# A planned lead-in: maxima taken by readiness, other TensorE times in the task list, dense groups let in earlier

## The chip, the cores and the metric

The kernel runs on one core of a Trainium2 chip. The metric is the device time of one execution in microseconds (us). The kernel before was run three times: 1574.43 us is the median, the runs lie between 1574.12 and 1575.43. One further execution was taken with the hardware profiler; its trace is what the views below show.

## What is computed

The input x has 2048 tokens of 512 numbers. One branch is attention in which 32 heads of 16 numbers share one key and one value head; the other is a feed-forward layer with the Mish function. All of it is in fp32.

```python
def _A_ref(x, wq, wk, wv, wo):                       # x: [1, 2048, 512]
    q = (x @ wq).reshape(B, S, H, Dh).transpose(0, 2, 1, 3)     # H = 32, Dh = 16
    k = x @ wk                                       # [1, 2048, 16], one for all heads
    v = x @ wv
    scores = jnp.einsum("bhqd,bkd->bhqk", q, k) * (Dh ** -0.5)
    p = _softmax(scores, axis=-1)
    o = jnp.einsum("bhqk,bkd->bhqd", p, v)
    return o.transpose(0, 2, 1, 3).reshape(B, S, H * Dh) @ wo
def _B_ref(x, w1, b1, w2):                           # 512 -> 1792 -> 512
    h = x @ w1 + b1
    return (h * jnp.tanh(softplus(h))) @ w2
xn = _layernorm(x)
return x + _A_ref(xn, wq, wk, wv, wo) * _silu(_B_ref(xn, w1, b1, w2))
```

## The kernel before

**Pieces.** The tokens are cut into four chunks of 512. A chunk's x is normalized, transposed by TensorE (tiles xp, L303), copied by ScalarE (xf), and projected to keys and values in four passes (kp, L341). ScalarE writes the high part of the keys, VectorE adds the low part (k_low, L238); from then on the chunk's keys are ready. ScalarE then copies the values (vt, L355), TensorE transposes them (vp, L360), and VectorE puts them in place. The queries come as 32 groups v of four heads times 512 queries, eight groups to a chunk.

**The loop.** It has 512 steps, one for each query group and tile of 128 keys. In a step TensorE makes four tiles of scores (e, L1056) which ScalarE turns into exponentials (pt, L1058), and it multiplies the exponentials of two steps ago with the values (four pv matmuls, L1143). The softmax needs the maximum of each query beforehand: for a later query group TensorE makes four further products (m, L1078), in each of which VectorE takes the maximum along 512 keys (mb, L1082). A query group has 32 *pairs* of these (one product from the upper and one from the lower half of the array's rows), and the maxima run LEAD = 20 steps ahead of the scores. When a group's 32 pairs are done, c_rows (L1097) reduces them and SyncE moves the result into the queries' spare rows with eight small DMAs (L1122); the group's scores need them.

**Dense work.** The query projection, the feed-forward layer and the output projection are cut into *groups*: a chain of matmuls into one bank of PSUM (xps), then a copy by ScalarE (hb, L763, for the feed-forward layer), which GpSimd works on. There is one such bank, so one group must be copied out before the next may begin. Within the loop a matmul is run as an upper and a lower row half (L120), up to eight halves in one step; ahead of the loop it is run whole (L116). A group can begin only when its weights have arrived and are split into high and low parts. Steps that find no group ready have no dense work.

**The lead-in.** What stands ahead of the loop is laid out when the program is built. A list of tasks (engine, assumed duration, what it depends on) is put into `plan`. Each engine has a clock T, and again and again the option that can start earliest is taken and its instructions are written out. For TensorE the options are a task from the list (x_transpose with an assumed 0.6 us at L1343, a pass of k_proj with 0.9 at L1378, v_transpose with 0.5 at L1389), "M" (one pair of maxima), or, if neither can start within 0.35 us, "X": three matmuls of a dense group. A new dense group is let in only while fewer than 1 + (s - 18) / X_US have begun at the assumed time s (L1480), and only when the copy of the last one has been written out; if none may begin, "X" is one warm-up matmul (keep_warm, L1393) that nobody reads. The copy of a finished group is itself a ScalarE task, put at 0.35 us after the group's last matmul (put_off, L1274). After "M" TensorE's clock is moved on by 0.25 or 0.45 (L1465).

Which pair "M" takes is a fixed list, MSEQ (L65): eight pairs of query group 0, two of group 1, the other 24 of group 0, the other 30 of group 1. m_ready (L1398) looks at the next entry only: its queries must have been moved, its chunk's keys be ready and a bank free. m_need (L69) says after how many pairs of the list a query group is complete. The loop begins once group 0's rows are moved and 40 pairs are done (L1454).

## Time and profile before

| what | value |
|---|---|
| median of three runs | 1574.43 us |
| the profiled execution's own span | 1575.7 us |
| TensorE (PE) busy | 1563.1 us, 99% of the span |
| VectorE (DVE) busy | 1352.7 us, 86% |
| ScalarE (ACT) busy | 1300.4 us, 83% |
| GpSimd (POOL) busy | 642.2 us, 41% |
| first score matmul of the loop | 82.58 us after the span's start |

A busy share is a mean over the lead-in, the loop and the end. A matmul's end is modelled, so a busy TensorE need not be one at its peak. PE is TensorE's matmuls, PEld its weight loads, SPq the DMA queue of SyncE. "Granted clock" is the share of TensorE's full clock that the chip gave it in a stretch. In the rows below, a bracket at the end of a row is the wait before it and the instruction that ended the wait.

### The profile page before, as it was taken

What the parts mean: (1) busy time and instruction counts of PE and PEld (TensorE: products, weight loads), DVE (VectorE), ACT (ScalarE), POOL (GpSimd) and SP (SyncE); (2) the same over time, 40 slices, a digit from 0 to 9 for tenths busy, and PEclk for the clock granted to TensorE, in tenths of its full rate; (3) what the DMA queues carried; (4) which work ended last, traced back from release to release, by engine and by line L of the source; (5) the groups of instructions that cost most, each with busy time, mean ns of one, the idle gap of its engine ahead of it and who ended that gap; (6) DMA issues with size and microseconds to landing.
All of it is one profiled execution on the core that took longest, in us unless ns stands there. A gap on an engine that the chain in (4) does not pass through costs nothing.

```text
span 1575.7 us, 32007 instructions
## 1 busy us (share of the span) xinstructions
PE 1563.1 (99%) x11905; PEld 846.9 (54%) x11905; DVE 1352.7 (86%) x2307; ACT 1300.4 (83%) x2501; POOL 642.2 (41%) x668
## 2 busy tenths in 40 slices
PE   8999999999999999999999999999999999999998
PEld 5555555555555555555555555555555555555555
DVE  7898888988989888898998988889889998888852
ACT  6488888798998778878888787887898879788876
POOL 4677376175474203604425042260442415225222
PEclk9999999999999999999999999999999999999999
DMA  6223132142331304122131311221413221031110
GB/s 196 94 85 118 52 102 104 42 141 85 111 103 46 110 20 143 51 69 75 31 102 51 125 58 43 85 70 38 144 59 105 59 94 65 19 111 32 48 44 29
DMA packets 75082, 124.45 MB, mean 79 GB/s; under 512 B 21744, under 2 KB 36336, under 8 KB 74928
## 3 DMA queue, kind: packets, MB, share of 16 engines
q1 hardware_dynamic: 74784, 122.29, 24.8%
q8 instruction: 94, 1.54, 0.4%
q14 instruction: 60, 0.49, 0.1%
q10 hardware_dynamic: 144, 0.13, 0.0%
HBM read 74.65 MB, written 26.21 MB: 64 GB/s over the span
## 4 chain that ended last, share of the span: by engine, by line
PE 96%; DVE 1%; ACT 1%; DMA 0%; issue 0%; SPq 0%; POOL 0%; DVEq 0%; ACTq 0%
PE xps L120 43%; PE pv L1143 32%; PE e L1056 10%; PE m L1078 7%; PE kp L341 1%; PE xps L116 1%; PE pv L1136 1%; DVE mb L1082 1%; PE e L1029 1%; PE tail L120 0%; PE tailx L120 0%; DMA xin<-in_dram 0%; ACT pt L1058 0%; ACT pt L1033 0%; PE tail L1231 0%
## 5 line engine op out<-in xcount | busy, mean ns | idle before, releaser
L1082 DVE TENSOR_REDUCE mb<-m 128x1 f32<-128x512 f32 x2048 | 1273.8, 683 | 168.7 <-PE m L1078 124.9
L1058 ACT ACTIVATE pt<-e 128x512 f32<-128x512 f32 x1978 | 1038.3, 601 | 215.3 <-PE e L1056 208.9
L1078 PE MATMUL m<-ks,qt 48*128 48x512 f32 (+1 forms) x2048 | 844.5, 422 | 0.7 <-DVE mb L1082 0.3
L1056 PE MATMUL e<-qt,ks 64*128 64x512 f32 x1978 | 722.4, 398 | 0.1
L1143 PE MATMUL pv<-pt,vaug 128*32 128x512 f32 x3968 | 528.5, 605 | 0.0
L1078 PEld LDWEIGHTS m<-ks,qt 48*128 48x128 f32 (+1 forms) x2048 | 373.5, 185 | 60.3 <-DVE mb L1082 18.1
L1056 PEld LDWEIGHTS e<-qt,ks 64*128 64x128 f32 x1978 | 367.5, 186 | 5.2 <-ACT pt L1058 1.1
L120 PE MATMUL xps<-xt,ws 64*128 64x512 f32 x1224 | 338.8, 409 | 0.0
L120 PE MATMUL xps<-wbs,act 64*128 64x512 f32 x1248 | 336.9, 407 | 0.1
L120 PEld LDWEIGHTS xps<-xt,ws 64*128 64x128 f32 x1224 | 210.9, 185 | 196.9 <-ACT pt L1058 129.1
L120 PEld LDWEIGHTS xps<-wbs,act 64*128 64x128 f32 x1248 | 217.7, 185 | 172.4 <-ACT pt L1058 109.1
L174 POOL TENSOR_SCALAR t<-t 128x512 f32<-128x512 f32 x56 | 34.4, 614 | 328.1 <-ACT t L771 327.8
L1143 PEld LDWEIGHTS pv<-pt,vaug 128*32 128x32 f32 x3968 | 78.1, 108 | 132.2 <-issue 124.0
L164 POOL TENSOR_TENSOR hb<-hb,t 128x512 f32<-128x512 f32 x56 | 72.3, 1290 | 97.1 <-ACT t L784 73.9
L120 PE MATMUL xps<-xt,wq 64*128 64x512 f32 x336 | 93.0, 410 | 0.0
L120 PEld LDWEIGHTS xps<-xt,wq 64*128 64x128 f32 x336 | 57.9, 185 | 54.1 <-ACT pt L1058 34.4
L120 PE MATMUL xps<-wbs,ot_all 64*128 64x512 f32 x288 | 79.5, 409 | 0.0
L120 PEld LDWEIGHTS xps<-wbs,ot_all 64*128 64x128 f32 x288 | 49.6, 184 | 46.7 <-ACT pt L1058 29.3
L164 POOL TENSOR_TENSOR hb<-hb,u 128x512 f32<-128x512 f32 x56 | 72.3, 1291 | 4.4
L164 POOL TENSOR_TENSOR act<-hb,act 128x512 fp32r<-128x512 f32 x56 | 72.1, 1287 | 4.7
L164 POOL TENSOR_TENSOR u<-u,t 128x512 f32<-128x512 f32 x56 | 71.8, 1282 | 4.7
L164 POOL TENSOR_TENSOR oc<-oc,sc 128x512 f32<-128x512 f32 x16 | 20.7, 1294 | 121.5 <-DMA wbs<-w 24.9
(160 smaller groups left out, 967.7 us busy)
## 6 DMA issues: line engine op xcount, KB each, us to landing
wbs<-w SPq DMA_DIRECT2D x36, 512.0 KB
ws<-w SPq DMA_DIRECT2D x35, 512.0 KB
qt<-qh SPq DMA_DIRECT2D x256, 32.0 KB
w<-wbs SPq DMA_DIRECT2D x14, 512.0 KB
w<-ws SPq DMA_DIRECT2D x14, 512.0 KB
wq<-wq SPq DMA_DIRECT2D x13, 512.0 KB
wbs<-wo SPq DMA_DIRECT2D x11, 512.0 KB
rawws<-in_dram SPq DMA_DIRECT2D x21, 256.0 KB
```

Source lines behind the costliest of these rows:

```text
L116: self.pe.matmul(ps, self.lhs(), self.rhs(), start=(self.k == 0), stop=(self.k == self.tot - 1))
L120: i = self.pe.matmul(ps, self.lhs()[o], self.rhs()[o], start=(self.k == 0 and self.halves == 0), stop=(self.k == self.tot - 1 and self.hal ...
L164: eng.tensor_tensor(out=o, in0=a, in1=b, op=op)
L174: pool.tensor_scalar(o, o, lim, 0.0, op0=ALU.min, op1=ALU.max)
L341: pe.matmul(kp_of[c], wkf[:, dt], xf_of[c][dt // 2][:, dt % 2], start=(dt == 0), stop=(dt == 3))
L1029: pe.matmul(es[a][:, C // 2 * m:C // 2 * (m + 1)], ks[o:o + 64, P * (k + m):P * (k + m + 1)], q[o:o + 64, i // 2, z], start=True, stop=True)
L1056: pe.matmul(e, ks[o:o + 64, P * k:P * (k + 1)], q[o:o + 64, p], start=True, stop=True)
L1058: r = act.activation(pt, e, AF.Exp, scale=0.25)
L1078: pe.matmul(m, q[o, p, P * t:P * (t + 1)], ks[o, C * kb:C * (kb + 1)], start=True, stop=True)
L1082: r = dve.reduce_max(out=mb_of[v][:, kb, z:z + 1], in_=m, axis=AX.X)
L1136: pe.matmul(o[32 * j:32 * j + 32, z], vaug[:, k + m], pts[j][:, C // 2 * m:C // 2 * (m + 1)], start=(k + m == 0), stop=(k + m == 15))
L1143: pe.matmul(o[32 * j:32 * j + 32], vaug[:, k], pt, start=(k == 0), stop=(k == 15))
```

## The change

It touches only the lead-in's planning. X_US goes from 13 to 9. The assumed TensorE times become 0.45 for the transpose of a tile, 0.86 for a pass of the key projection, 0.3 for the transpose of the values, and 0.35 in place of 0.45 for a pair of maxima that follows something else. The list MSEQ goes; m_ready looks at the next pair of query group 0 and of group 1, and takes the one that could start first, with 0.3 us of handicap for group 1. What was taken is kept in m_list, and group 0 is complete when none of its pairs is left. The loop's own code is the same.

```diff
--- before.py
+++ after.py
@@ -34,7 +34,7 @@
 LEAD = 20
 NWARM = 24
 E0 = 74
-X_US = 13.0
+X_US = 9.0
 A_LO = 12
 WAIT_US = 0.4
 KEEP_US = 6.0
@@ -62,13 +62,9 @@
 TERMS = ((0, 0), (0, 1), (1, 0))
 
 
-MSEQ = ([(0, n) for n in range(8)] + [(1, n) for n in range(2)]
-        + [(0, n) for n in range(8, 32)] + [(1, n) for n in range(2, 32)])
-
-
 def m_need(v):
 
-    return (34, 64)[v] if v < 2 else 32 * (v + 1)
+    return 32 * (v + 1)
 
 
 class Task:
@@ -1060,11 +1056,16 @@
         return r
 
     m_next = [0, 0]
+    m_list = []
+
+    def m_left(v):
+
+        return 32 - sum(u == v for u, n in m_list)
 
     rowq = deque()
 
     def m_one(a):
-        v, n = MSEQ[m_next[a]] if m_next[a] < 64 else divmod(m_next[a], 32)
+        v, n = m_list[m_next[a]] if m_next[a] < 64 else divmod(m_next[a], 32)
         m_next[a] += 1
         if v not in mb_of:
             mb_of[v] = sb.tile([P, 4, 16], F32, tag="mb", name=f"mb{v}", bufs=2)
@@ -1340,7 +1341,7 @@
             for t in range(4 * c, 4 * c + 4):
                 sc = task(*(("ACT", 0.72), ("DVE", 0.4))[c == 0 and t % 2], lambda t=t: x_scale(t), [nrm])
                 scs.append(sc)
-                tr = task("PE", 0.6, lambda t=t: x_transpose(t), [sc])
+                tr = task("PE", 0.45, lambda t=t: x_transpose(t), [sc])
                 if c == 0:
                     hi = task("ACT", 0.55, lambda t=t: x_high(t), [tr])
                     lo = task("DVE", 0.65, lambda t=t: x_low(t), [hi])
@@ -1375,7 +1376,7 @@
             if c == 0:
                 qp = task("PE", 2.8, q_first, xs[0:8:2] + xs[8:])
                 xs += [qp]
-            kus = 0.9
+            kus = 0.86
             k0 = kp = task("PE", kus, lambda c=c: k_proj(c, (0,)), xs)
             for dt in range(1, 4):
                 kp = task("PE", kus, lambda c=c, dt=dt: k_proj(c, (dt,)), [kp], lat=0.0)
@@ -1386,7 +1387,7 @@
             vc = task("ACT", 0.59, lambda c=c: v_copy(c), [kp], lat=0.7)
             bank("v", 1, k0, [kl, vc])
             lows.append((kp, kl))
-            vtr = task("PE", 0.5, lambda c=c: v_transpose(c), [vc])
+            vtr = task("PE", 0.3, lambda c=c: v_transpose(c), [vc])
             vo = task("DVE", 0.22, lambda c=c: v_out(c), [vtr])
             bank("v", 1, vtr, [vo])
 
@@ -1398,10 +1399,17 @@
     def m_ready(t):
         if min(m_next) >= 2 * LEAD or rows and rows[-1].end is None:
             return None
-        v, n = MSEQ[m_next[0]]
-        if len(qready.get(v) or ()) <= n % 8 // 4 or n // 8 not in kready:
+        found = []
+        for v in range(2):
+            n = 32 - m_left(v)
+            if n < 32 and len(qready.get(v) or ()) > n % 8 // 4 and n // 8 in kready:
+                found.append((max(t, qready[v][n % 8 // 4], kready[n // 8],
+                                  m_ends[-2 if not spare_e() else -5 if twin[0] else -3]) + 0.3 * v, v, n))
+        if not found:
             return None
-        return max(t, qready[v][n % 8 // 4], kready[n // 8], m_ends[-2 if not spare_e() else -5 if twin[0] else -3])
+        s, v, n = min(found)
+        m_pick[0] = (v, n)
+        return s - 0.3 * v
 
     def best(eng):
         found = None
@@ -1418,6 +1426,7 @@
         own = [kp.end + 0.8 for kp, kl in lows if kl.end is None and kp.end is not None]
         return min(own, default=10.0 ** 6)
 
+    m_pick = [None]
     begun = [0]
     twin = [False]
     rows = []
@@ -1457,15 +1466,16 @@
         for tag in items:
             load(tag)
         if k == "M":
+            m_list.append(m_pick[0])
             for a in range(2):
                 m_one(a)
             d = max(T["DVE"], s + 0.45)
             m_ends += [d + 0.6, d + 1.2]
             T["DVE"] = d + 1.2
-            T["PE"] = s + (0.25 if kind[0] == "M" else 0.45)
+            T["PE"] = s + (0.25 if kind[0] == "M" else 0.35)
             kind[0] = "M"
             twin[0] = spare_e() and not twin[0]
-            if vdone[0] == 0 and min(m_next) >= m_need(0):
+            if vdone[0] == 0 and not m_left(0):
                 vdone[0] = 1
                 r = c_rows(0)
                 r1 = task("DVE", 0.85, lambda r=r: (r[0](), r[1](), r[2]()), prio=-4)
@@ -1515,6 +1525,8 @@
         k.fn()
         k.end = now[0]
     lead.clear()
+    assert not m_left(0)
+    m_list.extend((1, n) for n in range(32 - m_left(1), 32))
     for k in range(NDT):
         at(20 + 8 * k, lambda k=k: xt_part(1, k))
```

In the program that comes out, 90 whole dense matmuls stand ahead of the loop where there were 75, and 14 single warm-up matmuls where there were 8; the number of maxima ahead of the loop is the same. Three places follow. In all of them m is a product for a maximum, with its half of the array's rows and its number after it; qt_77 are the queries of group 0 and qt_78 those of group 1.

TensorE between the second and the third chunk, before (xp transposes a tile of x, vp the values):

```order
L303 MATMUL xp_501<-ident,xin_1_145 128x128 x4
L360 MATMUL vp_514<-ident,vt_492 128x32 x4
L1078 MATMUL m_0_0_522<-ks,qt_78 128x512
L1078 MATMUL m_1_0_525<-ks,qt_78 128x512
L1078 MATMUL m_0_1_530<-ks,qt_78 128x512
L1078 MATMUL m_1_1_533<-ks,qt_78 128x512
L303 MATMUL xp_536<-ident,xin_2_147 128x128 x4
L303 MATMUL xp_541<-ident,xin_3_149 128x128 x4
L1078 MATMUL m_0_8_550<-ks,qt_77 128x512
L1078 MATMUL m_1_8_553<-ks,qt_77 128x512
L1078 MATMUL m_0_9_556<-ks,qt_77 128x512
L1078 MATMUL m_1_9_559<-ks,qt_77 128x512
```

The same place after (xps is a dense group, kp a pass of the key projection):

```order
L299 MATMUL xp_506<-ident,xin_2_147 128x128 x4
L356 MATMUL vp_513<-ident,vt_493 128x32 x4
L1079 MATMUL m_0_7_518<-ks,qt_77 128x512
L1079 MATMUL m_1_7_521<-ks,qt_77 128x512
L1079 MATMUL m_0_8_531<-ks,qt_77 128x512
L1079 MATMUL m_1_8_534<-ks,qt_77 128x512
L1079 MATMUL m_0_9_537<-ks,qt_77 128x512
L1079 MATMUL m_1_9_540<-ks,qt_77 128x512
L112 MATMUL xps<-xt_185,ws_304 128x512 x3
L299 MATMUL xp_548<-ident,xin_3_149 128x128 x4
L112 MATMUL xps<-xt_185,ws_304 128x512 x3
L337 MATMUL kp_563<-xf_0_502,wkf 128x512
```

Group 1's two pairs have left this place, and group 0's pairs and six matmuls of the first dense group stand among the tiles.

TensorE towards the end of the lead-in, before (names with their numbers: xps_907 and xps_948 are two dense groups in the one bank, m1 a product for query group 1):

```order
L116 MATMUL xps_907<-xt0_185,wbs_107 128x512 x9
L1078 MATMUL m1_0_5_927<-ks_98,qt1_78 128x512
L1078 MATMUL m1_1_5_930<-ks_98,qt1_78 128x512
L1078 MATMUL m1_0_6_933<-ks_98,qt1_78 128x512
L1078 MATMUL m1_1_6_936<-ks_98,qt1_78 128x512
L116 MATMUL xps_907<-xt0_185,wbs_107 128x512 x3
L116 MATMUL xps_948<-xt0_185,wbs_107 128x512 x3
L1078 MATMUL m1_0_7_952<-ks_98,qt1_78 128x512
L1078 MATMUL m1_1_7_955<-ks_98,qt1_78 128x512
L120 MATMUL xps_948<-xt0_185,wbs_107 128x512
L1078 MATMUL m1_1_8_959<-ks_98,qt1_78 128x512
```

The same place after (xps_879, xps_928 and xps_975 are three dense groups):

```order
L112 MATMUL xps_879<-xt0_185,wbs_107 128x512 x3
L112 MATMUL xps_928<-xt0_185,wbs_107 128x512 x3
L1079 MATMUL m1_0_4_935<-ks_98,qt1_78 128x512
L1079 MATMUL m1_1_4_938<-ks_98,qt1_78 128x512
L1079 MATMUL m1_0_5_948<-ks_98,qt1_78 128x512
L1079 MATMUL m1_1_5_951<-ks_98,qt1_78 128x512
L112 MATMUL xps_928<-xt0_185,wbs_107 128x512 x9
L112 MATMUL xps_975<-xt0_185,ws5_797 128x512 x3
L1079 MATMUL m1_0_6_979<-ks_98,qt1_78 128x512
L1079 MATMUL m1_1_6_982<-ks_98,qt1_78 128x512
L1079 MATMUL m1_0_7_985<-ks_98,qt1_78 128x512
L1079 MATMUL m1_1_7_988<-ks_98,qt1_78 128x512
```

Where one group's last matmuls stood directly before the next group's first ones once (907 and 948), it is so three times now; two of these three places are shown (879 and 928, 928 and 975).

TensorE in the loop's eighth step, before (e are scores, pv the product with the values, xps a dense half):

```order
L120 MATMUL xps<-xt_185,ws_736 128x512
L1078 MATMUL m_0_21_1253<-ks,qt_78 128x512
L120 MATMUL xps<-xt_185,ws_736 128x512
L1056 MATMUL e_0_1257<-qt_77,ks 128x512
L120 MATMUL xps<-xt_185,ws_736 128x512
L1078 MATMUL m_0_22_1262<-ks,qt_78 128x512
L120 MATMUL xps<-xt_185,ws_736 128x512
L1056 MATMUL e_1_1266<-qt_77,ks 128x512
L120 MATMUL xps<-xt_185,ws_736 128x512
L1078 MATMUL m_0_23_1271<-ks,qt_78 128x512
L120 MATMUL xps<-xt_185,ws_736 128x512
L1056 MATMUL e_2_1277<-qt_77,ks 128x512
```

The same step after:

```order
L1079 MATMUL m_1_21_1293<-ks,qt_78 128x512
L1052 MATMUL e_0_1296<-qt_77,ks 128x512
L1079 MATMUL m_1_22_1300<-ks,qt_78 128x512
L1052 MATMUL e_1_1303<-qt_77,ks 128x512
L1079 MATMUL m_1_23_1307<-ks,qt_78 128x512
L1052 MATMUL e_2_1310<-qt_77,ks 128x512
L1079 MATMUL m_1_24_1314<-ks,qt_78 128x512
L1052 MATMUL e_3_1317<-qt_77,ks 128x512
L1144 MATMUL pv_1106<-pt_2_1236,vaug 32x512
```

The six dense halves of this step are gone; so it is in four steps of the loop, the 8th, 17th, 18th and 139th.

## Rows read from the trace of the kernel before

**Rows 1.** The page's chain that ended last: shares of the span by engine

```profile
PE 96%; DVE 1%; ACT 1%; DMA 0%; issue 0%; SPq 0%; POOL 0%; DVEq 0%; ACTq 0%
```

**Rows 2.** The chain in order of time, two stretches of the loop: start, us, what

```profile
101.18 1.03 PE pv L1143 x8
...
104.03 1.02 PE pv L1143 x8
...
144.42 1.00 PE pv L1143 x8
...
147.47 0.99 PE pv L1143 x8
```

**Rows 3.** TensorE in order of time, end of the lead-in: start, us, line, shape, count, wait

```profile
66.42 1.67 PE L116 MATMUL xps<-xt,ws 128*128 128x512 f32 x6
...
68.81 1.66 PE L116 MATMUL xps<-xt,ws 128*128 128x512 f32 x6
...
79.31 0.96 PE L116 MATMUL xps<-xt,wbs 128*128 128x512 f32 x3
...
81.14 0.93 PE L116 MATMUL xps<-xt,wbs 128*128 128x512 f32 x3 [0.87 <-ACT hb L763]
...
82.58 0.39 PE L1056 MATMUL e<-qt,ks 64*128 64x512 f32 x1
```

**Rows 4.** VectorE in order of time: start, us, line, operation, shape, count, wait before it

```profile
45.05 2.48 DVE L1082 TENSOR_REDUCE mb<-m 128x1 f32<-128x512 f32 x4 [2.77 <-PE m L1078]
...
48.71 0.75 DVE L238 SCALAR_TENSOR_TENSOR ks<-ks,ksgn,kp 112x512 fp32r<-112x512 f32 x1 [1.18 <-ACT vt L355]
...
51.90 8.57 DVE L1082 TENSOR_REDUCE mb<-m 128x1 f32<-128x512 f32 x14
...
61.47 0.75 DVE L238 SCALAR_TENSOR_TENSOR ks<-ks,ksgn,kp 112x512 fp32r<-112x512 f32 x1 [1.00 <-ACT vt L355]
...
76.40 14.61 DVE L1082 TENSOR_REDUCE mb<-m 128x1 f32<-128x512 f32 x24
```

**Rows 5.** Busy time of each engine by stretch, then granted clock, DMA share, GB/s

```profile
core 0: us, PE busy (x) PEld busy (x) DVE busy (x) ACT busy (x) POOL busy (x), PEclk, DMA share, GB/s
...
38.50:45.40 6.90, 6.90 (x17) 2.64 (x15) 3.71 (x7) 3.10 (x9) 2.63 (x8) 0.51 0.71 237
...
49.00:53.70 4.70, 4.33 (x29) 2.58 (x25) 4.70 (x9) 4.68 (x11) 0.07 (x1) 1.00 0.00 0
...
70.00:80.00 10.00, 9.93 (x43) 6.13 (x41) 9.86 (x21) 4.40 (x7) 8.28 (x10) 1.00 0.01 1
```

**Rows 6.** TensorE in order of time, 35 to 47 us

```profile
35.71 0.43 PE L360 MATMUL vp<-ident,vt 32*128 32x32 f32 x4 [0.71 <-DVE ks L238]
...
36.07 0.81 PE L1078 MATMUL m<-ks,qt 64*128 64x512 f32 x4
...
38.21 0.82 PE L303 MATMUL xp<-ident,xin 128*128 128x128 f32 x4 [0.75 <-ACT xf L327]
...
38.97 1.61 PE L1078 MATMUL m<-ks,qt 64*128 64x512 f32 x4
...
40.51 3.78 PE L341 MATMUL kp<-xf,wkf 128*128 128x512 f32 x4
...
44.22 1.22 PE L1078 MATMUL m<-ks,qt 64*128 64x512 f32 x4
...
45.37 1.99 PE L341 MATMUL kp<-xf,wkf 128*128 128x512 f32 x4
```

**Rows 7.** SyncE's queue at the end of the lead-in

```profile
76.54 5.34 SPq L1122 DMA_DIRECT2D qt<-cr  x8
```

**Rows 8.** ScalarE in order of time, the copy of a dense group

```profile
80.31 0.69 ACT L763 ACTIVATE hb<-xps,b1c 128x512 f32<-128x512 f32 x1 [2.34 <-PE xps L116]
```

**Rows 9.** GpSimd in order of time, the first dense group

```profile
55.10 0.61 POOL L174 TENSOR_SCALAR t<-t 128x512 f32<-128x512 f32 x1 [6.04 <-ACT t L771]
...
57.84 1.27 POOL L164 TENSOR_TENSOR hb<-hb,u 128x512 f32<-128x512 f32 x1
```

## The prediction

> **What bounds the kernel now.** I read the page's chain first, then windows, then the lead-in queue by queue, because only the lead-in is edited. TensorE is 96% of the chain that ended last [rows 1]. In the loop a step lasts 2.85 us from one pv to the next (101.18 to 104.03), and 3.05 us (144.42 to 147.47) where it carries eight dense half matmuls instead of six [rows 2]; so a pair of halves that leaves a loop step is worth about 0.2 us, and nothing that merely lets another engine finish sooner is worth anything there.
>
> The lead-in ends with the first score matmul, at 82.58 [rows 3]. In it two engines are level. VectorE's maxima cost 0.60 each when they follow one another: 14 in 8.57, 24 in 14.61 [rows 4]. TensorE needs 2.39 for six dense and four maxima matmuls (66.42 to 68.81) [rows 3], and four maxima take VectorE 4 x 0.60 = 2.40. Between 70 and 80 both are full: 9.93 and 9.86 of 10 us [rows 5]. Taking work from one of them there is worth nothing without the other.
>
> VectorE's longest hole is the 2.77 before 45.05 [rows 4]. TensorE made it: after two waits of 0.71 and 0.75 its granted clock was down to one half (0.51 from 38.5 to 45.4, that is 1.2 for 2.4 GHz) [rows 5, 6], and four passes of the key projection took 3.78, against 1.99 once the clock was back [rows 6]. Against the full-speed rows this cost (1.61 - 0.81) + (3.78 - 1.99) + (1.22 - 0.81) = 3.0 us [rows 6].
>
> **The change part by part.** Removed: nothing but the fixed list. Each maximum is still one TensorE and one VectorE instruction, and 81 maxima matmuls stand ahead of the first score in both programs. *The order of the maxima* turns out to change little: query group 1 loses its two pairs after group 0's eighth and gets four pairs between group 0's 24th and 25th. Group 0's 32nd pair is therefore the 36th, not the 34th, in the row, and four pairs, not six, are left behind it. A pair costs 1.2 wherever it stands. On SyncE the eight small DMAs of group 0's rows, 5.34 long [rows 7], keep their place behind the same 53 others; what moves is when VectorE hands them over.
>
> *The corrected TensorE times and the earlier dense groups* move the rest. 90 full dense matmuls stand ahead of the loop, not 75, and 14 single warm-up matmuls, not 8. The dense ones cost TensorE 15 x 0.235 = 3.5 (six take 2.39 less about 1.0 for the four maxima and two switches [rows 3]); the warm-up ones fill waits and cost 0 to 1.4, of which I take 0. A second price is hidden in the order. All dense groups share one PSUM bank, so where one group's last three matmuls stand directly before the next group's first three, TensorE waits for ScalarE's copy (0.69) [rows 8]: 79.31 to 81.14 is 1.83, less 3 x 0.235, so 1.1 per such seam [rows 3]. Before there is one seam, now there are three: + 2.2. Against this stand the 3.0 of the half clock, if TensorE now stays at full speed, and the waits of 0.71 + 0.75 [rows 6] that dense matmuls can fill: - 4.5. Balance: 3.5 + 2.2 - 4.5 = + 1.2. On GpSimd the first dense group's four operations (55.10 to 59.1, so 4.0 [rows 9]) now stand ahead of the fourth chunk's norm. With that group's copy at about 39.5 they end by 44.5 and the norm by 48, a microsecond before its transposes are due; only if GpSimd is later than that does the fourth chunk pay, one for one.
>
> I walk it by stages as a check. *To the third chunk's low keys* (48.71 before [rows 4]): without the 3.0, about 45.7, with the six extra dense matmuls that stand there (1.4) in the holes. 14 pairs are reduced by then in both orders. *To the fourth* (61.47 before): 12 pairs stand between instead of nine, 24 x 0.60 = 14.4, the low keys 0.66, a copy 0.13, and waits. The new order has two transposes through one bank and waits for scaled tiles there; I take 1.3, between 0 (as in the gapless rows from 51.90 [rows 4]) and the 2.77 of the worst hole: 45.7 + 16.5 = 62.2. That is 0.7 late, but 26 pairs are done, not 23, so VectorE is ahead by 3 x 1.2 - 0.7 = 2.9. *To the first score*: from there TensorE sets the time. After the value transpose (1.2 from the low keys) stand 45 dense matmuls (10.6), six sets of four maxima with their switches (6.0), three seams (3.3) and 0.5 to the score: 62.2 + 21.6 = 83.8, against 82.58. The 2.9 are given back: with 12 dense matmuls and a seam between group 1's sixth and seventh pairs, VectorE runs out of maxima. The rows of group 0 would be handed over at about 77.3, against 76.54 [rows 7], and the score that needs the first four of its DMAs comes 6.4 later, no sooner after it than before (6.0); no new wait. Lead-in: + 1.2 (the steps at the loop's head then need 2.4 each of VectorE in both).
>
> *The loop.* 15 matmuls are 30 halves less, but they don't come out evenly. Counting matmuls of each row half between pv groups, four early steps now have no dense work at all (the 8th, 17th, 18th and 139th), because the next weights aren't split yet, others have eight or an uneven pair, and the tail gains two lone stretches. The longer side of every step, summed, falls from 3647 to 3642 matmul times of 0.21, that is by 1.1 us: 1.5 less in the steps before the last twenty, 0.4 more in those. An empty step would be 2.22 by TensorE, but VectorE's four maxima need 2.4, so I give back 0.2 to 0.4 for each of the four: loop - 0.2.
>
> **Sum** against the profiled execution, span 1575.7: + 1.2 - 0.2 = + 1.0. The span is 1.3 above the median of the runs, so I move the difference to the median: 1574.43 + 1.0 = 1575.4.
>
> **A rule against the change.** Between 33 and 39 TensorE had little but transposes, and the clock fell [rows 6]; between 49.0 and 53.7 it also had mostly transposes and the clock held at 1.00 [rows 5]. In the new order transposes stand as thickly at both places (four tiles and the value transpose with four pairs of maxima before the fourth tile of the third chunk). The Trainium skill ("TensorE: Matmul & The Clock Gate", Part 4: PE-mode transpose) says a transpose doesn't count as PE-busy the way a matmul does. By that, the first stretch agrees and the second doesn't; it is the third rival below.
>
> **The rivals.** *VectorE's lead is kept* (the other way, faster): if the seams cost nothing and TensorE keeps pace, the 2.9 carry to the loop: 1574.4 - 2.9 - 0.2 = 1571.3. It decides at group 1's seventh pair, which must be issued by about 79. For it: TensorE's busy time is partly modelled. Against it: the seam at 81.14 is a real wait of 0.87 [rows 3]. *The moved matmuls are paid back in full*: 30 halves x 0.1 = 3.0 off the loop instead of 0.2, so 1575.4 - 2.8 = 1572.6. For it: every loop step hangs on TensorE [rows 2]. Against: the count of longer sides. *The clock falls again* (slower than before): one fall costs the 3.0 measured here, 1575.4 + 3.0 = 1578.4; it decides if the half clock again lies on key projections and maxima that VectorE is waiting for, at either of the two places named above. For it: the same mix of work. Against: dense and warm-up matmuls now stand among them, and the clock held through the second place before [rows 5]. *The change doesn't do what it says*: the ready order hardly differs from the list, so if its price and the dense groups' cancel, it is the median again, 1574.4; this lies inside the forecast's own range of 1573.6 to 1577.2.
>
> **How the numbers follow.** Chances: the forecast with the cancelling case 0.55, the kept lead 0.15, paid back in full 0.13, the clock falling 0.17. A measurement of this kernel can tell 0.2% from no change, that is 3.15 us: below 1571.28 is faster, above 1577.58 slower. The kept lead is centred on that bound, so 0.6 of it counts as faster, 0.2 of the paid-back case, a little of the forecast: 0.14. The clock case gives 0.13 of slower, the forecast's upper end and a longer wait at the fourth chunk 0.06: 0.19. The rest, 0.67, is no change. The range leaves out a tenth on each side: half of the kept lead below 1571.5, the far half of the clock case above 1578.3. The costs that no row shows (warm-up 0 to 1.4, waits 0 to 2.8 at the fourth chunk, empty steps 0 to 1.6) lie inside it.
>
> **What would show it.** Right: granted clock 1.00 throughout 30 to 60, the third low keys near 45.7 and the fourth near 62; three waits of about 0.9 of dense matmuls on ScalarE's copy between 67 and 81; a hole of 2 us and more in VectorE's maxima near 79 to 82; the first score between 83 and 84.5; empty steps of 2.4 to 2.6. Wrong: a first score before 81.5 (the lead was kept), a clock of 0.5 anywhere in the lead-in, or loop steps from the 30th on that are shorter than their count says.

## The result

The changed kernel takes 1579.77 us (median of six runs, 1579.22 to 1580.64) against 1574.21 for the kernel before (six runs, 1573.79 to 1575.43): a ratio of 1.0031 with the interval 1.002 to 1.0041, so 5.6 us slower by the medians and 4.9 by the ratio. A second set, on another occasion, gave 1580.57 against 1574.81, 1.0036 (1.0022 to 1.0049). Two executions further down stand far from all others (3591.41 in `times_no_warm`, 2893.78 in `after_late_copy`), and the medians of their kernels are given without them. The prediction was 1575.4 in a range of 1571.5 to 1578.3: no change was forecast, and the time lies above the range.

The page of the changed kernel (span; busy time and share of each engine; chain that ended last):

```profile
span 1578.8 us, 32041 instructions
...
PE 1563.8 (99%) x11896; PEld 844.9 (54%) x11896; DVE 1353.4 (86%) x2307; ACT 1302.0 (82%) x2502; POOL 639.7 (41%) x665
...
PE 97%; DVE 1%; ACT 1%; SPq 0%; issue 0%; DMA 0%; POOL 0%; DVEq 0%; ACTq 0%; POOLq 0%
```

Nothing in it tells the story: the shares are those of before, and TensorE's is 97% of the chain where it was 96% [rows 1]. VectorE in order of time in the lead-in (start, us, line, shape, count, and in brackets the hole before it):

```profile
42.33 5.06 DVE L1083 TENSOR_REDUCE mb<-m 128x1 f32<-128x512 f32 x8 [2.49 <-PE m L1079]
47.52 0.75 DVE L234 SCALAR_TENSOR_TENSOR ks<-ks,ksgn,kp 112x512 fp32r<-112x512 f32 x1
...
64.81 0.75 DVE L234 SCALAR_TENSOR_TENSOR ks<-ks,ksgn,kp 112x512 fp32r<-112x512 f32 x1
...
73.76 4.88 DVE L1083 TENSOR_REDUCE mb<-m 128x1 f32<-128x512 f32 x8 [0.74 <-PE m L1079]
...
84.02 8.46 DVE L1083 TENSOR_REDUCE mb<-m 128x1 f32<-128x512 f32 x14 [2.04 <-PE m L1079]
```

TensorE at the end of the lead-in (the waits for ScalarE's copies stand in brackets):

```profile
72.32 0.98 PE L112 MATMUL xps<-xt,wbs 128*128 128x512 f32 x3 [0.69 <-ACT qf L703]
...
77.96 0.93 PE L112 MATMUL xps<-xt,wbs 128*128 128x512 f32 x3 [0.87 <-ACT hb L759]
...
82.58 0.97 PE L112 MATMUL xps<-xt,ws 128*128 128x512 f32 x3 [0.78 <-ACT hb L759]
...
85.38 0.39 PE L1052 MATMUL e<-qt,ks 64*128 64x512 f32 x1
```

The first score stands at 85.38; it was at 82.58 [rows 3]. The low keys of the third chunk come at 47.52, of the fourth at 64.81 (48.71 and 61.47 before [rows 4]). The three waits that the prediction named are there (0.69, 0.87, 0.78), and behind the first and the last of them VectorE has holes of 0.74 and 2.04. In this execution too TensorE fell to half clock, for a shorter time (window, busy time of each engine, granted clock):

```profile
37.00:41.00 4.00, 4.00 (x13) 2.80 (x13) 2.83 (x6) 1.45 (x5) 0.00 (x0) 0.64 0.46 148
```

### The profile page after: what moved, and what is told of

The parts are those of the page before. It is cut to its first block, busy times and chain, and to the rows that moved or that the text cites. A ratio compares the mean times of both kernels' runs of the same rounds, so it can differ in the third digit from the quotient of the medians.

```text
span 1578.8 us, 32041 instructions
## 1 busy us (share of the span) xinstructions
PE 1563.8 (99%) x11896; PEld 844.9 (54%) x11896; DVE 1353.4 (86%) x2307; ACT 1302.0 (82%) x2502; POOL 639.7 (41%) x665
## 4 chain that ended last, share of the span: by engine, by line
PE 97%; DVE 1%; ACT 1%; SPq 0%; issue 0%; DMA 0%; POOL 0%; DVEq 0%; ACTq 0%; POOLq 0%
PE xps L116 44%; PE pv L1144 31%; PE e L1052 9%; PE m L1079 6%; PE xps L112 1%; PE kp L337 1%; DVE mb L1083 1%; PE pv L1137 1%; PE warm L1312 1%; SPq L1164 0%; PE e L1025 0%; PE xp L299 0%; PE tail L116 0%; PE warm L1397 0%; PE tail L1232 0%
## 5 line engine op out<-in xcount | busy, mean ns | idle before, releaser
L116 PE MATMUL xps<-wbs,ot_all 64*128 64x512 f32 x306 | 84.2, 407 | 0.0
L116 PEld LDWEIGHTS xps<-wbs,ot_all 64*128 64x128 f32 x306 | 52.6, 185 | 47.2 <-ACT pt L1054 29.3
```

Source lines behind the costliest of these rows:

```text
L116: i = self.pe.matmul(ps, self.lhs()[o], self.rhs()[o], start=(self.k == 0 and self.halves == 0), stop=(self.k == self.tot - 1 and self.hal ...
```

## Experiments

The kernel before was run beside each. Over all experiments that makes 131 executions with their mean granted clock: 72 at 1.000 (median 1574.97), 24 at 0.999 (1575.06) and 35 at 0.997 (1577.72).

### The kernel before once more

No edit.

> The kernel before, unchanged, profiled once more. Its profiled execution had a span of 1575.7 us and 7 us of half clock, but its runs have a median of 1574.2, while an execution of the changed kernel takes 1.7 us more than its own span; so the profiled execution was about 3.2 us slower than the runs. Theory (the half clock was an accident of that execution): the runs show a clock of 1.000 and spans near 1572.5, and a new trace has no stretch at half clock between 35 and 47, with the first score at 82.6 - 3.0 = 79.6. Rival (the half clock belongs to this order of work): clock 0.997 in every run, and the first score again at 82.6. By the time alone: 1574.2 in both.

Measured: 1575.31, ratio 1.0004 (0.9995 to 1.0013). The new trace has a span of 1573.5 and full clock. VectorE and TensorE in it, in the rows that answer to [rows 3, 4, 6], with the handover of group 0's rows (cr, the last operation of c_rows) at 73.32, and a window from 35 to 47 with the granted clock third from the end:

```profile
42.29 2.48 DVE L1082 TENSOR_REDUCE mb<-m 128x1 f32<-128x512 f32 x4 [0.68 <-PE m L1078]
45.78 0.75 DVE L238 SCALAR_TENSOR_TENSOR ks<-ks,ksgn,kp 112x512 fp32r<-112x512 f32 x1 [1.00 <-ACT vt L355]
...
58.53 0.75 DVE L238 SCALAR_TENSOR_TENSOR ks<-ks,ksgn,kp 112x512 fp32r<-112x512 f32 x1 [1.00 <-ACT vt L355]
...
73.32 0.21 DVE L1114 STREAM_TRANSPOSE cr<-mp 128x32 f32<-128x32 f32 x1
73.46 14.61 DVE L1082 TENSOR_REDUCE mb<-m 128x1 f32<-128x512 f32 x24
```

```profile
39.85 1.98 PE L341 MATMUL kp<-xf,wkf 128*128 128x512 f32 x4
...
79.65 0.39 PE L1056 MATMUL e<-qt,ks 64*128 64x512 f32 x1
```

```profile
35.00:47.00 12.00, 10.54 (x47) 5.54 (x48) 10.32 (x18) 7.91 (x21) 5.76 (x11) 1.00 0.59 206
```

The hole of 2.77 is one of 0.68, the four key matmuls from 39.85 take 1.98 (3.78 at half clock [rows 6]), and the first score is at 79.65, 2.9 earlier (0.3 of it was there at the first low keys). Five of these 11 executions were at 0.997, and 35 of the 131. So the half clock belongs neither to every execution nor to none: it is a draw of about one in four, it costs 2.7, and the median of the runs doesn't contain it. The one profiled execution that I had, did.

### One part at a time

`ready_only` keeps the ready order and takes back the rest; with the old times a limit of 13 or 9 gives the same program. `times_only` is the kernel before with the four new times. `list_x9` is that with the limit of 9 too, so the changed kernel with the fixed list. The three other times go with the one shown.

```diff
 ready_only, against the changed kernel
-X_US = 9.0
+X_US = 13.0
-tr = task("PE", 0.45, lambda t=t: x_transpose(t), [sc])
+tr = task("PE", 0.6, lambda t=t: x_transpose(t), [sc])
...
 times_only, against the kernel before
-tr = task("PE", 0.6, lambda t=t: x_transpose(t), [sc])
+tr = task("PE", 0.45, lambda t=t: x_transpose(t), [sc])
...
 list_x9, against the kernel before
-X_US = 13.0
+X_US = 9.0
-tr = task("PE", 0.6, lambda t=t: x_transpose(t), [sc])
+tr = task("PE", 0.45, lambda t=t: x_transpose(t), [sc])
...
```

> The kernel before with one part of the change: the next pair of maxima is chosen by readiness; the assumed TensorE times are the old ones (the limit of 13 or 9 makes no difference then: the program is the same). 75 whole dense matmuls stand ahead of the loop and one direct seam between dense groups, as before. Theory (the loss is TensorE's time for more dense matmuls and for waits at seams): 1574.2 within 0.7. Rival (the order of the maxima itself costs, because group 1's pairs now stand between group 0's): most of the 5.6, so 1578 to 1580.

Measured: 1575.24, ratio 0.9999 (0.999 to 1.0008). The order of the maxima costs nothing and brings nothing. It does what it says, though: group 0's rows are handed over three earlier than the 73.32 of the kernel before, and the first score is not earlier.

```profile
70.31 0.21 DVE L1115 STREAM_TRANSPOSE cr<-mp 128x32 f32<-128x32 f32 x1
```

```profile
79.51 0.39 PE L1052 MATMUL e<-qt,ks 64*128 64x512 f32 x1
```

> The kernel before with only the assumed TensorE times changed; fixed list, limit 13. 84 whole dense matmuls ahead of the loop (9 more), no direct seam (one fewer). Theory (dense matmuls 0.235 each, seams 1.1 each, nothing given back by the loop): 1574.2 + 2.1 - 1.1 = 1575.2. Rival (the order of the maxima costs): 1574.2. Second rival (the new times make the plan follow the chip better, as the lead kept by VectorE would have it): under 1573.

> The changed kernel with the fixed list put back: new times, limit 9, 90 whole dense matmuls ahead of the loop as in the changed kernel, but no two dense groups directly behind one another. Theory (dense 0.235 each, seams 1.1 each): 1574.2 + 3.5 - 1.1 = 1576.6, that is 3.3 below the changed kernel at 1579.8. Rival (the order of the maxima costs): 1574.2. Second rival (the number of dense matmuls alone decides, seams cost nothing): 1579 to 1580, like the changed kernel.

Measured: 1579.27, ratio 1.0023 (1.0015 to 1.0032), and 1579.54, ratio 1.0025 (1.0015 to 1.0034). My theory of that time, 0.235 per dense matmul and 1.1 per seam, falls: with nine and with fifteen more dense matmuls the loss is the same, and neither has two groups directly behind one another. So the new TensorE times alone carry most of the loss. What they have in common shows in a window laid from the first chunk's low keys to the first pv; in each line VectorE's busy time is the one with about 104 instructions. The kernel before (new trace, with the columns), the changed kernel, `times_only` and `list_x9`:

```profile
core 0: us, PE busy (x) PEld busy (x) DVE busy (x) ACT busy (x) POOL busy (x), PEclk, DMA share, GB/s
21.95:86.77 64.82, 60.42 (x267) 33.41 (x265) 59.32 (x104) 39.12 (x83) 37.76 (x48) 1.00 0.34 108
```

```profile
21.59:92.37 70.78, 65.02 (x284) 35.54 (x283) 59.87 (x104) 43.73 (x92) 44.01 (x54) 0.98 0.31 101
```

```profile
22.48:90.54 68.06, 63.80 (x288) 35.35 (x287) 59.77 (x104) 43.91 (x93) 44.94 (x55) 1.00 0.34 110
```

```profile
22.13:89.36 67.23, 63.25 (x284) 35.33 (x283) 59.78 (x105) 43.92 (x93) 43.96 (x54) 1.00 0.34 111
```

VectorE's work is the same in all, 59.3 to 59.9; the stretches differ (64.82, 70.78, 68.06, 67.23) by what VectorE is idle in them (5.50, 10.91, 8.29, 7.45). That alone doesn't make VectorE the one that sets the time: it has the same work in all four, so its busy time must be the same. By these rows it could be TensorE too, whose busy time in the last two is 3.4 and 2.8 above the 60.42 of the first, with nearly the same idle time (4.40, 4.26, 3.98). Against that, the growth doesn't follow the nine and fifteen matmuls added. The next two experiments give work to one engine at a time.

### Which engine sets the lead-in

`dve_plus` makes a small copy ten times instead of once, `pe_plus` a dense matmul five times.

```diff
 dve_plus
+        for _ in range(10 if c == 3 else 1):
             dve.tensor_copy(vaug[:, 4 * c:4 * c + 4, 0:DH], vp_of[c][:, :, 16:32])
 pe_plus
                 begun[0] += fresh
+                for _ in range(4 if fresh and begun[0] == 3 else 0):
+                    g0 = cur["g"].mms[0]; pe.matmul(cur["ps"], g0.lhs(), g0.rhs(), start=True, stop=True)
```

> The kernel before with nothing but nine more copies on VectorE, ahead of the maxima that follow the fourth chunk's low keys: the small copy of the values is made ten times instead of once, 9 x 0.13 = 1.2 us of VectorE, nothing on TensorE. Theory V (VectorE sets the end of the lead-in: in six traces the stretch from the first low keys to the first pv is 59.3 to 59.9 us plus VectorE's idle time): the whole 1.2 appears, 1576.2 against 1575.0, and VectorE's idle time in that stretch stays 5.5. Theory T (TensorE's work sets it, as the sum of the prediction had it): no change, 1575.0.

> The kernel before with nothing but four more matmuls on TensorE, 4 x 0.235 = 0.94 us: the first matmul of the third dense group is run five times (the last one counts), between maxima at about 61. Theory V (VectorE sets the end, and it has one or two maxima in stock there): 0 to 0.3, so 1575.0 to 1575.3. Theory T (each dense matmul ahead of the loop costs its 0.235): the whole 0.94, 1576.0.

Measured: `dve_plus` 1577.88, ratio 1.0015 (1.0006 to 1.0024); `pe_plus` 1575.67, ratio 0.9998 (0.999 to 1.0007). The copies cost more than I had put (61.36 - 59.32 = 2.04, so 0.23 each), and the runs show the whole of it. The stretch from the first low keys to the first pv in `dve_plus`, then in `pe_plus`, then in the first trace of before:

```profile
21.91:88.58 66.67, 60.52 (x267) 33.30 (x265) 61.36 (x113) 39.13 (x83) 37.74 (x48) 1.00 0.34 105
```

```profile
22.59:90.40 67.81, 63.34 (x271) 34.33 (x269) 59.44 (x104) 39.12 (x83) 37.80 (x48) 0.95 0.33 104
```

```profile
22.21:89.71 67.50, 63.31 (x268) 34.44 (x266) 59.39 (x104) 39.08 (x83) 37.64 (x48) 0.95 0.33 104
```

TensorE's 0.94 don't show in the runs, though their interval reaches to 1.1. The trace settles it: it has the half clock at the same place as the first trace of before (0.51 from 38.8 to 45.7, the same hole of 2.77), and against that one its stretch is 0.3 longer. So in the kernel before, at these two places, VectorE sets the time, and TensorE's work counts only where it makes VectorE wait. In the changed kernel that wasn't tried.

### Fewer dense matmuls, and the warm-up matmuls

```diff
 x_us_20, against the kernel before
-X_US = 13.0
+X_US = 20.0
```

> The kernel before with fewer dense groups let in: X_US 20 instead of 13, 60 whole dense matmuls ahead of the loop instead of 75, and 23 single warm-ups instead of 8. Theory V (VectorE's holes alone count; the loop takes the 30 halves back at 0.02 each, as the changed kernel's loop shows the other way round): 1575.0 to 1575.5. Theory T (0.235 per dense matmul ahead of the loop): 3.5 off and 0.4 back in the loop, 1571.9.

Measured: 1578.24, ratio 1.0019 (1.001 to 1.0028): slower, as neither theory had it. TensorE, the weight load of the second warm-up, VectorE, and a window (the number behind the last engine is the granted clock):

```profile
74.36 4.72 PE L1396 MATMUL warm<-qt 128*128 128x512 f32 x9 [1.05 <-DVE mb L1082]
```

```profile
74.91 0.19 PEld L1396 LDWEIGHTS warm<-qt 128*128 128x128 f32 x1 [0.36 <-PE warm L1396]
```

```profile
79.84 2.48 DVE L1082 TENSOR_REDUCE mb<-m 128x1 f32<-128x512 f32 x4 [2.55 <-PE m L1078]
```

```profile
76.00:80.00 4.00, 3.92 (x10) 2.05 (x10) 1.45 (x4) 0.00 (x0) 3.83 (x4) 0.57 0.02 3
```

Nine warm-up matmuls take 4.72, 0.52 each where a dense one takes 0.235, since each load waits for the warm-up before it (0.36); the first waited for VectorE to empty a bank, because keep_warm writes into one of the maxima's three. VectorE starves for 2.55 behind them. And they don't hold the clock: 0.57 in their last part.

The next three leave out the warm-ups behind the first query projection, in `x_us_20`, in `times_only` and in the changed kernel:

```diff
-                keep_warm()
+                if s < 19.5:
+                    keep_warm()
                 T["PE"] = s + 0.25
```

> The kernel before with X_US 20 and without the later warm-ups. With them it took 1576.8 at full clock for most of the lead-in, and nine warm-ups in a row (4.72 from 74.36, 0.55 each, at a granted clock of 0.57 towards their end) stood ahead of a hole of 2.55 in VectorE's maxima. Theory W: that hole is gone and the time near that of the kernel before, 1574.3 to 1575.3. Rival (the clock falls there for want of work): 1577 or more. Theory T (fewer dense matmuls are worth 0.235 each): under 1573.

Measured: 1576.75, ratio 1.0007 (0.9998 to 1.0016). The hole is gone: 17 maxima in a row where there were six, a hole of 2.55 and four. But all its executions are at 0.995 to 0.997, with half clock in the loop's first steps:

```profile
73.49 10.26 DVE L1082 TENSOR_REDUCE mb<-m 128x1 f32<-128x512 f32 x17
```

```profile
78.00:82.00 4.00, 3.88 (x13) 1.76 (x11) 4.00 (x8) 1.66 (x3) 3.44 (x4) 0.51 0.11 26
```

> The new times alone (fixed list, limit 13) with the single warm-up matmuls behind the first query projection left out; the plan, and so everything else in the program, is as in that kernel, which took 1578.4 in its runs at full clock. In its trace 12 warm-ups take 5.27 us instead of 12 x 0.235, and one row of five (2.71 from 79.0) stands ahead of VectorE's hole of 0.83. Theory W (a warm-up is written into one of the three banks of the maxima, so it waits for VectorE, and the next maxima wait for it): the holes of 0.58, 0.94 and 0.83 shrink, 1.0 to 2.0 off, 1576.5 to 1577.4. Rival (warm-ups only fill time that TensorE has anyway): 1578.4. Second rival (without them TensorE falls to half clock): 1579.5 or more.

> The changed kernel without the later warm-ups (seven single ones behind the first query projection). In its trace they take 2.63 us, 0.99 more than 7 x 0.235, around the holes of 0.56 and 0.95. Theory W: 0.5 to 1.0 off, 1578.5 to 1579. Rival: 1579.5, as the changed kernel.

Measured: 1578.98, ratio 1.002 (1.0011 to 1.0029), and 1581.52, ratio 1.0035 (1.0021 to 1.0049). In the first the holes of 0.57, 0.94 and 0.83 are 0.33, 0.66 and none, but a granted clock of 0.64 between 24 and 28 makes the first hole 3.30. In the second 0.50 between 55 and 60 makes a hole of 3.02 of one of 0.95. Both effects show: warm-ups take VectorE's banks, and without them the clock fell more often (`times_only` was at 0.999 to 1.000 in every execution, without warm-ups at 0.995 to 0.999). In these two they cancel or worse.

### The seams, and dense work in small gaps

`after_seam` lets a dense group begin only when the last one's copy has ended, and plans that copy 0.9 instead of 0.35 behind the last matmuls; `after_gap` puts dense work only into gaps of over 0.75.

```diff
 after_seam, against the changed kernel
+    copies = []
+    def bank_free(s):
+        return not copies or copies[-1].end is not None and copies[-1].end + 0.1 <= s
...
-        t = task("ACT", 0.69, fn, at=now[0] + lead.get("late", 0.35))
+        t = task("ACT", 0.69, fn, at=now[0] + lead.get("late", 0.9))
+        copies.append(t)
...
-            if cur["g"] is not None or not waiting and begun[0] < 1 + (s - 18) / X_US and begin():
+            if cur["g"] is not None or bank_free(s) and begun[0] < 1 + (s - 18) / X_US and begin():
 after_gap, against the changed kernel
-        if e0 is None or e0[0] > T["PE"] + 0.35:
+        if e0 is None or e0[0] > T["PE"] + 0.75:
```

> The changed kernel, with the plan made to know that the one bank is taken until ScalarE's copy has ended: a dense group begins only 0.1 us after that, and the copy is put 0.9 instead of 0.35 us after the group's last three matmuls begin. 78 whole dense matmuls ahead of the loop instead of 90, more warm-ups (26 instead of 14), no two groups directly behind one another. Theory V: the two holes of VectorE that stand behind seams in the changed kernel's trace (0.74 and 2.04) go, the others stay: about 2.8 less than the changed kernel, so near 1577. Theory T: 12 dense matmuls fewer (2.8) and three seams fewer (3.3), 1579.8 - 6.1 = 1573.7. Rival (what the new assumed times do earlier costs everything): 1579.5.

Measured: 1579.44, ratio 1.0023 (1.0014 to 1.0032). In the lead-in it went as expected: both holes are gone and VectorE is idle for 7.2 instead of 9.3 (the changed kernel's second trace, below). But from the first pv to the 30th the trace loses 1.4 against that of before: two steps take 3.36 and 3.38 instead of 2.85, because a dense group waits there for its weights on GpSimd, and others are fuller. So the loop's head took back most of the 2.2 that the lead-in gained.

> The changed kernel with one number of the plan changed: three dense matmuls or a warm-up are put in only where TensorE could start nothing else within 0.75 us, instead of 0.35. With the new, shorter times the plan sees gaps of 0.35 to 0.75 in which it puts 0.7 us of dense work, and what comes after it, often a pair of maxima, is late. 75 whole dense matmuls ahead of the loop, as before, two direct seams. Theory (the loss is VectorE's holes, made by dense work in small gaps): the holes of 1.73, 0.56, 0.95 and 2.04 shrink and the time is back at 1575 to 1576. Rival (the loss lies in the new order of transposes and projections that the times bring): 1578 to 1579.5.

Measured: 1577.23, ratio 1.0013 (1.0004 to 1.0022): of the loss some 2 are left, so 3 or more are gone. It has 75 dense matmuls, as before; but `times_only` and `list_x9` have shown that their number alone doesn't decide. The first hole is back at 1.03, the last is 0.62, but there is a new one, at half clock; none of its executions is at 1.000.

```profile
52.08 2.48 DVE L1083 TENSOR_REDUCE mb<-m 128x1 f32<-128x512 f32 x4 [2.59 <-PE m L1079]
```

```profile
50.00:52.00 2.00, 2.00 (x8) 1.00 (x6) 0.00 (x0) 1.93 (x4) 0.00 (x0) 0.50 0.00 0
```

### The late norm of the fourth chunk

```diff
 after_late_copy, against the changed kernel
-        t = task("ACT", 0.69, fn, at=now[0] + lead.get("late", 0.35))
+        t = task("ACT", 0.69, fn, at=max(now[0] + lead.get("late", 0.35), 0 if now[0] < 20 else 46.5))
```

> The changed kernel, with the copy of its first dense group of the feed-forward layer put off to 46.5 us of the plan; in its trace that copy (40.4) and GpSimd's four operations behind it (41.9 to 45.9) stand ahead of the fourth chunk's sums and norm, which ends at 49.8 instead of 44.8. 81 whole dense matmuls ahead of the loop, three direct seams still. Theory V: the fourth low keys come 4 to 5 earlier than at 64.8, but VectorE had group 1's pairs to fill that time, so only the holes around 52 to 60 change (1.5 in sum), and the seams' 2.8 stay: 1578.5 to 1579.5. Rival N (the late norm is the cause of the loss): 1575 to 1576.5.

Measured: 1579.88, ratio 1.0024 (1.0014 to 1.0034). GpSimd in the changed kernel, with the first dense group's operations ahead of the norm, and the norm's end in the new trace of before:

```profile
41.86 0.61 POOL L170 TENSOR_SCALAR t<-t 128x512 f32<-128x512 f32 x1 [5.61 <-ACT t L767]
...
44.60 1.28 POOL L160 TENSOR_TENSOR hb<-hb,u 128x512 f32<-128x512 f32 x1
...
49.64 0.20 POOL L269 TENSOR_TENSOR nbias<-nbias,rstd 128x4 f32<-128x4 f32 x1
```

```profile
44.62 0.20 POOL L273 TENSOR_TENSOR nbias<-nbias,rstd 128x4 f32<-128x4 f32 x1
```

The norm ends five later in the changed kernel. With the copy put off, the fourth low keys come 2.5 earlier, counted from the first, than in the changed kernel's second trace (39.2 against 41.6), and VectorE is idle for the same 9.3. The late chunk costs next to nothing, because VectorE has group 1's pairs in the meantime.

### Letting the loop in earlier

`list_early` begins the loop after 36 pairs, and makes up the four in the third, fifth, seventh and ninth step. `ready_early` does that in the changed kernel, with both edits of the section on seams. `ready_low` lets one more pair stand ahead of each low key. `lead_18` keeps the maxima 18 steps ahead.

```diff
 list_early, against the kernel before
-        if min(m_next) >= 2 * LEAD or rows and rows[-1].end is None:
+        if min(m_next) >= 36 or rows and rows[-1].end is None:
...
-        if cdone[0] is not None and s >= cdone[0] - 0.4 and min(m_next) >= 2 * LEAD:
+        if cdone[0] is not None and s >= cdone[0] - 0.4 and min(m_next) >= 36:
...
             waves(h, em, inm)
+            if s in (2, 4, 6, 8):
+                m_one(0)
+                m_one(1)
 ready_low, against ready_only
-        if m is not None and max(T["DVE"], m + 0.45) + 1.2 > low_due() + 0.5:
+        if m is not None and max(T["DVE"], m + 0.45) + 1.2 > low_due() + 1.1:
 lead_18, against the kernel before
-LEAD = 20
+LEAD = 18
```

> The kernel before, fixed list, with the loop let in after 36 pairs of maxima instead of 40; the four pairs are made up in the third, fifth, seventh and ninth step. In the trace of the kernel before group 0's rows are handed over at 73.3 and the first score stands 6.3 later, so the rows and not the 40 pairs should hold the loop's start. Theory: no gain at the first score, 4 x 0.2 lost in the loop, 1575.0 to 1575.8. Rival (the 40 pairs hold the start): up to 2.4 less, 1572.6 to 1573.5.

> The changed kernel with three things more: dense work only in gaps over 0.75 us, a dense group begun only when the bank has been copied out, and the loop let in after 36 pairs instead of 40, made up in the third to ninth step. In the trace of the ready order alone group 0's rows were handed over at 70.3, three earlier than in the kernel before, and yet the first score stood at 79.5, because the loop waited for 40 pairs. Theory: that lead is now used, first score 2 to 3 us earlier, less 0.8 in the loop: 1573 to 1573.5, ahead of both kernels. Rival (the first score hangs on something else, such as TensorE's own work): 1575 or later.

Measured: 1577.13, ratio 1.0013 (1.0004 to 1.0022), and 1577.57, ratio 1.0012 (1.0003 to 1.0022). For `list_early` my theory was wrong at both ends. Group 0's rows didn't hold the start: they are handed over at 72.97, as before, and the first score came at 77.82, 1.8 earlier. And a pair made up in the loop costs 0.8, not 0.2: the first pv is 1.5 ahead of before, ten steps later the trace is 1.7 behind, with three steps of 3.92. In `ready_early` the first score came at 77.37, 2.3 ahead of before, as expected; there only the loop's price was wrong. A step has 2.85, four maxima take VectorE 2.48, six take 3.68:

```profile
72.97 0.21 DVE L1114 STREAM_TRANSPOSE cr<-mp 128x32 f32<-128x32 f32 x1
...
78.05 8.58 DVE L1082 TENSOR_REDUCE mb<-m 128x1 f32<-128x512 f32 x14 [2.50 <-PE m L1078]
...
89.75 3.68 DVE L1082 TENSOR_REDUCE mb<-m 128x1 f32<-128x512 f32 x6 [0.32 <-PE m L1078]
```

> The ready order with the old times (1575.2), with one number of the plan changed: a pair of maxima may be put ahead of a chunk's low keys on VectorE if the low keys are then at most 1.1 us late, instead of 0.5. One more pair stands ahead of the low keys of the second to fourth chunk. Theory V: the holes of 0.99, 1.00 and 1.00 in front of the low keys are filled with maxima, at up to 0.3 each of later keys: 1575.2 - 2 to - 3, so 1572.5 to 1573.2. Theory T: TensorE has the same work, 1575. Rival (later low keys move a hole elsewhere): 1574.5 to 1576.

Measured: 1576.27, ratio 1.0006 (0.9997 to 1.0014). The holes ahead of the low keys (0.99, 1.00 and 1.00) are none, 0.71 and none, but every execution is at 0.997 to 0.999, and the trace has a hole of 3.25 at a granted clock of 0.50. Whether the order would gain at full clock stays open.

> The kernel before with LEAD 18 instead of 20: the loop begins after 36 pairs of maxima and the maxima stay 18 steps ahead of the scores, so nothing is made up. Theory V: first pv 1.5 earlier, as with the loop let in early, 1.0 more in the loop and its end (3652 against 3647 matmul times of 0.21), so 1574.3 to 1574.8 at full clock. Rival (a group's maxima are then complete two steps, 5.7 us, ahead of its first score instead of four, and the rows' way through SyncE took 6.3): a wait at each of 31 query groups, 1580 or much more.

Measured: 1622.67, ratio 1.0301 (1.0287 to 1.0315). The rival was right, and the clock is at most a small part of it: it is 1.00 in the trace from 90 to 1500. The chain at one of its query groups (start, us, what): the last maximum, SyncE's small DMAs, and a score that waited for them.

```profile
316.48 0.65 DVE mb L1082
317.23 0.65 SPq L1122
...
318.58 1.65 DMA qt<-cr
320.27 0.49 PE e L1056
```

### The changed kernel once more

> The changed kernel, unchanged, profiled once more. Its first trace had 3 us of half clock around 39, with a hole of 2.49 in VectorE's maxima where the same place in a kernel with the fixed list and the same times has 0.90. Theory V: an execution without the half clock has its third low keys at 46.0 instead of 47.5, VectorE idle for 9.3 instead of 10.9 from the first low keys to the first pv, first score near 83.8 and first pv near 90.8, and the runs at full clock are at 1579.0 to 1579.8, 4.0 to 4.6 above those of the kernel before at full clock. Rival (the half clock belongs to the changed order): the same hole again.

Measured: 1580.57 against 1574.81, as told above. The trace is at full clock, and has the holes again, but for the one of 2.49, which is 0.90:

```profile
26.30 5.02 DVE L1083 TENSOR_REDUCE mb<-m 128x1 f32<-128x512 f32 x8 [1.74 <-PE m L1079]
...
42.02 5.07 DVE L1083 TENSOR_REDUCE mb<-m 128x1 f32<-128x512 f32 x8 [0.90 <-PE m L1079]
...
53.45 4.92 DVE L1083 TENSOR_REDUCE mb<-m 128x1 f32<-128x512 f32 x8 [0.55 <-PE m L1079]
59.32 5.06 DVE L1083 TENSOR_REDUCE mb<-m 128x1 f32<-128x512 f32 x8 [0.95 <-PE m L1079]
...
73.45 4.88 DVE L1083 TENSOR_REDUCE mb<-m 128x1 f32<-128x512 f32 x8 [0.73 <-PE m L1079]
...
83.70 8.46 DVE L1083 TENSOR_REDUCE mb<-m 128x1 f32<-128x512 f32 x14 [2.03 <-PE m L1079]
```

```profile
22.87:92.06 69.19, 63.45 (x284) 34.45 (x283) 59.88 (x104) 43.70 (x92) 43.97 (x54) 1.00 0.32 102
```

So the half clock in the first trace was no cause of the loss.

## Why the prediction was wrong

**The step that failed** is the balance "3.5 + 2.2 - 4.5 = + 1.2", and in it the credit of 4.5. Of it 3.0 were the half clock of the profiled execution, which the median never contained. The sign stood in the numbers I had: the span of 1575.7 was longer than any of the three runs (1575.43 at most), though a run takes longer than its span (1580.54 to 1578.8 in the changed kernel, 1575.28 to 1573.5 in the new trace of before). That execution was some 3 above the median, not 1.3, and I compared a walk at full clock with a first score that had half clock in it. The other 1.5 were waits of TensorE that dense matmuls would fill. They mostly did (0.71 became 0.27, 0.75 is gone), and VectorE got nothing from it: its hole behind them was 0.68 at full clock before and is 0.90. Without the credit the sum is 1574.4 + 5.7 - 0.2 = 1579.9. (The 3.0 itself is near what the runs gave, 2.7. Its first term set the maxima beside a row without waits; the same three rows at full clock are 1.31, 1.98 and 0.74, so 2.6. And the four key matmuls of such a row are two passes, not four: the trace has eight to a chunk.)

**That this is the measured time is partly luck.** The 5.7 were TensorE's price for dense matmuls and seams, and `pe_plus` shows 0.3 of 0.94 for four matmuls more, `x_us_20` no gain from fifteen fewer. In the two traces at full clock the stretch from the first low keys to the first pv grew from 64.8 to 69.2, by 4.4: 3.8 are VectorE's idle time (5.5 to 9.3). The holes of it: 0.7 more ahead of the first maxima (three dense matmuls stand there now), 0.4 in the three next, 0.5 less at the third and fourth low keys, 2.8 behind the seams, 0.4 in gaps under 0.3 each. The rest of the 4.4 is 0.6 of VectorE's own work. 0.9 more came before the stretch, where the changed kernel's two traces differ by 1.3 among themselves. What made the holes is in the main the new assumed times (`times_only`): with them the plan sees gaps of over 0.35 and puts dense work or a warm-up into them, and the maxima behind come late. `after_gap`, which asks for 0.75, loses 2 instead of 5.6; as every execution of it has some half clock, its worth at full clock stays open.

**"Two engines are level"** was the reading behind it. Both were near 100% from 70 to 80 [rows 5], and a busy TensorE can contain waits (the nine warm-ups of `x_us_20` fill 4.72); VectorE's rows without gaps [rows 4] were the sign of who made whom wait, and adding work to one engine at a time showed it.

**Point by point.** *Order of the maxima changes little*: right, 0.9999. *Seams, 1.1 each*: the waits were there; in VectorE's terms two of three counted, 0.73 and 2.03. *Warm-ups, 0 to 1.4, taken as 0*: about 0.5 by the two holes that shrank in `times_no_warm` (0.57 and 0.94 to 0.33 and 0.66), which stand in the changed kernel too (0.55 and 0.95); in `x_us_20` warm-ups made a hole of 2.55. *GpSimd*: the norm ended at 49.8, not 48, and ScalarE waited 0.9 for it; as the runs show, that cost next to nothing. *The walk*: third low keys 45.7 forecast and 47.2 at full clock, fourth 62.2 and 64.5, first score 83.8 and 85.1; 0.9 of each was there at the first low keys. *The loop, - 0.2*: from the first pv to the end it was 0.0 at full clock: 0.4 less up to the 488th step, 0.4 more in the tail, as the count had it. An empty step saves 0.14, not 0.25 to 0.45: it lasts 2.71, because between its first maxima TensorE waits for VectorE (the chain):

```profile
129.61 0.99 PE pv L1144 x8
...
131.08 0.69 DVE mb L1083
...
132.32 1.00 PE pv L1144 x8
```

**The rivals.** *VectorE's lead is kept* and *paid back in full* (faster): neither, the first score came 5.4 later. *The clock falls again*: it did in the first trace, for 1.6 of VectorE's time, but the second trace is as slow without it; its 1578.4 had the right sign for the wrong reason. The Trainium skill ("TensorE: Matmul & The Clock Gate", Part 4: PE-mode transpose) has transposes not counting as PE-busy the same way; here the very same order of instructions, with the same transposes ahead of it, was at 0.51 from 38.5 to 45.4 in one execution and at 1.00 from 35 to 47 in the next, so the order alone doesn't decide it; something that differs between executions does, and it stays open what. Part 1 of that page ("What's actually happening") does say that the number of slow matmuls at a kernel's start differs between runs of the same kernel; the 35 of 131 are such a difference too, and the two traced executions of this order at 0.997 (before and `pe_plus`) have it in the middle of a stage.

## What to carry to other kernels

Hold the profiled execution against the runs before any row of it enters a sum: a span longer than every run's time means that the trace contains something that the median doesn't. Where two engines look full, give each in turn a little more work and nothing else: the one whose work shows whole sets the stretch, and a change is priced by the holes that it makes or closes there, not by instructions. Comparing busy and idle times over traces doesn't tell it, since an engine with the same work has the same busy time in any of them. A planner whose assumed times are put right can lose, where the old ones had left room that the real waits needed; here the new gaps were filled with work ahead of the engine that was the bound.

## What was not expected of the hardware

- One program, two clocks: TensorE's mean clock fell to 0.997 in 35 of 131 executions of the kernel before, 2.7 us each (7 us at half clock in the one traced ahead of the prediction); in `x20_no_warm`, `ready_low` and `after_gap` no execution was at 1.000.
- Nine warm-up matmuls in a row ran 0.52 apart instead of 0.235, and the granted clock was 0.57 in their last part.
- Two steps of margin (5.7) for a handover that takes VectorE's reduction, SyncE's DMAs and 1.65 of landing are too few: `lead_18` lost 47 us over 31 query groups, and 29 such landings stand in its chain.
- No version here beats the kernel before. Its remaining 5.5 of VectorE's idle time in the lead-in are holes of 0.5 to 1.03; the attempts to close them let the clock fall or moved them into the loop's head.
